# Loading the first halves of k and v through ScalarE's DMA queue

## The chip, the cores and the metric

The kernel runs on one core of one Trainium2 chip. A core has five engines with an instruction stream each: TensorE (matrix products, PE in the profile, its weight loads PEld), VectorE (DVE), ScalarE (ACT), GpSimd (POOL) and SyncE (SP). Transfers between device memory and the on-chip memory run on 16 DMA engines; an instruction of SyncE or of ScalarE issues them, and the profile shows these issues as SPq and ACTq. The metric is the device time of one execution in microseconds. Lower is better.

## What is computed

Two parts follow each other. The first is a linear attention with a cosine weight (cosFormer), for 8 batches, 8 heads, 576 positions and 64 features per head:

```python
theta = pi / 2 * arange(S) / S
phi(x) = concat(relu(x) * cos(theta), relu(x) * sin(theta))   # 64 -> 128 features
kv  = einsum('bhsf,bhsd->bhfd', phi(k), v)
z   = sum over positions of phi(k)
num = einsum('bhsf,bhfd->bhsd', phi(q), kv)
den = einsum('bhsf,bhf->bhs',  phi(q), z) + 1e-6
x   = (num / den), heads side by side: 4608 x 512
```

The second is a feed-forward layer on these 4608 rows: `h = x @ w_in` (512 to 2048), `g = max(0.01 h, h)`, `out = g @ w_out` (2048 to 512). Inputs and output are float32; the kernel multiplies in float16.

## The kernel before

The positions of a batch are split into 512 main ones (4 per partition, on 128 partitions) and a tail of 64. Each batch goes through the same steps: load q, k and v; build the features of k and q (`k_part`, `q_part`, on VectorE or ScalarE); form kv and its column of sums on TensorE (`kv_mm`); transpose the features of q; multiply them with kv and divide (`num_half`, `divide`); transpose the result x; and run the two products of the feed-forward layer over it. Batch 0 and batch 1 are written out by hand, from batch 2 on a list sorted by position (`line`, `put`) sets the order, with seven products in place of eight for 2 x 2 blocks of the feed-forward layer. Nothing reorders the program: each engine works through its instructions in the order in which they are written, and waits where an input is not there.

The change concerns the start. There all loads stand on SyncE, in this order: q of batch 0 in two halves (four heads each), first half of k, first half of v, the tails of k and of v (two transfers each), second half of k, second half of v, then eight transfers of w_in, and w_out and batch 1 after them. A half is 128 partitions x 4 heads x 4 positions x 64 features in float32, 512 KB.

While these are under way, TensorE runs 28 blank matmuls (`idle(14, ps_idle)`, line 169). VectorE and ScalarE prepare constants: the tables cos_t and sin_t (ScalarE, lines 214 and 215) are a column of every q and k feature. Then the order written out by hand for batch 0 is:

- VectorE: the features of q's first four heads (positions j = 0 and 2), of the second four heads (the same), of all heads for j = 3; then the features of k's first four heads for j = 0 to 2, the copy of v's first four heads to float16 (`v_main`), the features of k's tail, one half of v's tail.
- ScalarE: the features of q for j = 1, two copies of transposed q out of PSUM, the features of k's first four heads for j = 3, one half of v's tail, a third copy, and the copy of kv (`kv_half`, line 322).
- TensorE: the transposes of q (`q_transpose`, line 365, each over all eight heads), with blank matmuls after the first two; 18 blank matmuls; kv of the first four heads (lines 289 and 298); then, after the copy of kv, `num_half`, the same for the second four heads, the transposes of x and the first product of the feed-forward layer (`ffn1`, line 459).
- GpSimd: the copy of v's second four heads, then most of the casts of w_in to float16 (line 248).

The staging buffers of q, k and v for batch 0 (`stage`, three buffers) are given on to w_out's first two quarters and to batch 1's q once they have been read. ScalarE issues no DMA before the stores at the very end of the kernel.

Of the kernel before, what the change touches and what calls it, by code (L numbers as in the profile page):

```python
# [18 lines left out]
def kernel(  # L19
# [14 lines left out]
    nc = tc.nc  # L34
# [45 lines left out]
    ACT, DVE, POOL = nc.scalar, nc.vector, nc.gpsimd  # L80
# [3 lines left out]
    def staged(shape, name, soon=False):  # L84
        p, tag = (early, "early") if soon else (stage, "stage")
        return p.tile(shape, dt.float32, name=name, tag=tag)

    def load_main(nm, src, b, parts=(0, 1), soon=False):

        if parts[0] == 0:  # L90
            st[nm, b] = staged([P, H, J, D], f"{nm}st", soon)
        lo, hi = 4 * parts[0], 4 * parts[-1] + 4
        nc.sync.dma_start(
            st[nm, b][:, lo:hi],
            src[b, lo:hi, 0:MAIN, :].rearrange("h (p j) d -> p h j d", j=J),
        )

    def load_kvtail(nm, src, b):

        t = kvtail.tile([P, H // 2, D], dt.float32, name=f"{nm}tl", tag="kvtail")  # L100
        v4 = src[b, :, MAIN:S, :].rearrange("(c o) p d -> o p c d", o=2)
        for o in range(2):
            nc.sync.dma_start(t[o:P:2], v4[o])
        st[nm + "t", b] = t
# [10 lines left out]
    def load_k(b):  # L115
        load_main("k", k, b)
        load_kvtail("k", k, b)

    def load_v(b):
        load_main("v", v, b)  # L120
        load_kvtail("v", v, b)
# [20 lines left out]
    def load_w2(i):  # L142
        t = staged([P, 4, DM], "w2st", i > 1)
        nc.sync.dma_start(t, w2v[i])
        st["w2", i] = t

    load_main("q", q, 0, (0,))
    load_main("q", q, 0, (1,))
    load_main("k", k, 0, (0,))
    load_main("v", v, 0, (0,))  # L150
    load_kvtail("k", k, 0)
    load_kvtail("v", v, 0)
    load_main("k", k, 0, (1,))
# [943 lines left out]
    for b in range(2, NG):  # L1097
        at_, eng, s0 = AT[min(b, 5)], ENG[min(b, 5)], top[b] if b > 3 else 0
# [53 lines left out]
```

## Time and profile before

| what | value |
|---|---|
| median of 3 runs | 272.06 us |
| lowest and highest | 271.58 and 272.49 us |
| profiled execution, span from first to last instruction | 272.0 us |
| TensorE busy | 264.6 us (97%) |
| VectorE, ScalarE busy | 201.0 us, 200.7 us (74% each) |
| bytes moved by DMA | 57.05 MB, mean 210 GB/s |
| granted TensorE clock | 1.000 of full speed |

The page gives no other time of the profiled execution than its span. In a row of the order of time stand the start in us, the duration in us, the engine, the line of the kernel, the operation, the output and inputs by name, their shapes, how many instructions were merged (x8), and in brackets the idle time of the engine before it and what ended that. In a row of a table by stretches stand the stretch, its length, busy time and count of an engine, the granted clock, the mean busy share of the DMA engines and GB/s. In a row of DMA issues stand what is loaded, the issuing queue, the count, the size of one and the time from issue to landing.

### The profile page before, as it was taken

What the parts mean: (1) busy time and instruction counts of PE and PEld (TensorE: products, weight loads), DVE (VectorE), ACT (ScalarE), POOL (GpSimd) and SP (SyncE); (2) the same over time, 40 slices, a digit from 0 to 9 for tenths busy, and PEclk for the clock granted to TensorE, in tenths of its full rate; (3) what the DMA queues carried; (4) which work ended last, traced back from release to release, by engine and by line L of the source; (5) the groups of instructions that cost most, each with busy time, mean ns of one, the idle gap of its engine ahead of it and who ended that gap; (6) DMA issues with size and microseconds to landing.
All of it is one profiled execution on the core that took longest, in us unless ns stands there. A gap on an engine that the chain in (4) does not pass through costs nothing.

```text
span 272.0 us, 6597 instructions
## 1 busy us (share of the span) xinstructions
PE 264.6 (97%) x2660; PEld 226.8 (83%) x2660; DVE 201.0 (74%) x444; ACT 200.7 (74%) x331; POOL 10.1 (4%) x21
## 2 busy tenths in 40 slices
PE   8999999999999999999999999999999999999994
PEld 5876555665898979889999999999999989999983
DVE  5774589797986797899779696978577757645652
ACT  6756556696878898798899789978966657766621
POOL 1055101000000000000000000000000000000000
PEclk9999999999999999999999999999999999999999
DMA  6999989998999959997999699967274312200314
GB/s 228 318 374 413 398 291 361 368 267 254 309 208 342 175 178 264 312 172 228 259 280 161 183 276 275 181 212 155 62 149 144 61 41 96 80 0 2 154 39 118
DMA packets 87150, 57.05 MB, mean 210 GB/s; under 512 B 56656, under 2 KB 82256, under 8 KB 86608
## 3 DMA queue, kind: packets, MB, share of 16 engines
q1 hardware_dynamic: 86816, 56.37, 78.1%
q8 instruction: 21, 0.34, 0.5%
q10 hardware_dynamic: 304, 0.26, 0.4%
q14 instruction: 9, 0.07, 0.1%
HBM read 36.70 MB, written 9.44 MB: 170 GB/s over the span
## 4 chain that ended last, share of the span: by engine, by line
PE 69%; DMA 3%; DVE 2%; ACT 2%; issue 1%; ACTq 0%; DVEq 0%
PE ps_o L890 31%; PE ps_h L785 27%; PE ps_h L495 3%; DMA qst<-in_q_dram 3%; PE ps_h L890 3%; PE ps_num L380 2%; PE ps_kv L289 2%; DVE gs L254 1%; PE ps_kv L298 0%; ACT g L798 0%; PE ps_xt L445 0%; ACT g L812 0%; DVE xw L254 0%; ACT qp L238 0%; DVE xs L396 0%
## 5 line engine op out<-in xcount | busy, mean ns | idle before, releaser
L890 PEld LDWEIGHTS <-g 128*128 128x128 f16 x640 | 62.5, 98 | 7.3 <-DVE g L251 0.2
L251 DVE TENSOR_TENSOR u<-ps_h,u 128x512 f32<-128x512 f32 x52 | 35.8, 688 | 25.7 <-PE ps_h L785 22.9
L890 PE MATMUL ps_o<-w,g 128*128 128x256 f16 x352 | 51.2, 273 | 0.0
L785 PEld LDWEIGHTS <-w 128*128 128x128 f16 x416 | 44.5, 114 | 1.2
L785 PE MATMUL ps_h<-xT,w 128*128 128x256 f16 x288 | 43.3, 273 | 0.0
L785 PEld LDWEIGHTS <-wa 128*128 128x128 f16 x312 | 34.0, 113 | 2.0 <-DVE xw L254 0.9
L812 ACT ACTIVATE g<-u 128x1024 f16<-128x1024 f32 x26 | 27.5, 1058 | 10.9 <-DVE u L251 10.8
L798 ACT ACTIVATE g<-ps_h 128x512 f16<-128x512 f32 x52 | 31.2, 602 | 5.7 <-PE ps_h L785 5.7
L805 ACT COPY u<-ps_h 128x512 f32<-128x512 f32 x52 | 30.4, 585 | 5.4 <-PE ps_h L785 5.4
L890 PE MATMUL ps_o<-wb,g 128*128 128x256 f16 x232 | 33.5, 273 | 0.0
L785 PE MATMUL ps_h<-xw,wa 128*128 128x256 f16 x208 | 31.3, 273 | 0.6 <-DVE xw L254 0.6
L890 PEld LDWEIGHTS <-gs 128*128 128x128 f16 x256 | 24.9, 98 | 2.9
L908 ACT COPY ob<-ps_o 128x512 f32<-128x512 f32 (+1 forms) x32 | 17.9, 561 | 9.2 <-PE ps_o L890 9.0
L495 PE MATMUL ps_h<-xT,w 128*128 128x512 f16 (+1 forms) x104 | 24.7, 363 | 0.0
L396 DVE TENSOR_TENSOR xs<-ps_num,rden 128x512 f16<-128x512 f32 x28 | 19.4, 691 | 1.0
L890 PE MATMUL ps_o<-w,gs 128*128 128x256 f16 x120 | 17.8, 273 | 0.0
L251 DVE TENSOR_TENSOR ob<-ps_o,ob 128x512 f32<-128x512 f32 (+1 forms) x22 | 14.9, 675 | 3.7 <-ACT ob L908 1.4
L890 PE MATMUL ps_o<-wb,gs 128*128 128x256 f16 x120 | 17.5, 273 | 0.0
L254 DVE TENSOR_TENSOR gs<-g 128x1024 f16<-128x1024 f16 x16 | 11.0, 689 | 8.3 <-ACT g L812 8.1
L795 ACT COPY ps_h<-ps_h 128x512 f32<-128x512 f32 x26 | 14.9, 572 | 2.0 <-PE ps_h L785 1.1
L785 PE MATMUL ps_h<-xw,w 128*128 128x256 f16 x104 | 15.6, 273 | 0.0
L785 PE MATMUL ps_h<-xT,wa 128*128 128x256 f16 x104 | 15.6, 273 | 0.0
(113 smaller groups left out, 408.6 us busy)
## 6 DMA issues: line engine op xcount, KB each, us to landing
qst<-in_q_dram SPq DMA_DIRECT2D x7, 1024.0 KB, 7.0
out_dram<-ob SPq DMA_DIRECT2D x14, 512.0 KB, 2.8
kst<-in_k_dram SPq DMA_DIRECT2D x6, 1024.0 KB, 8.3
vst<-in_v_dram SPq DMA_DIRECT2D x6, 1024.0 KB, 7.1
w1st<-in_moe_w_in_dram SPq DMA_DIRECT2D x8, 512.0 KB, 9.4
w2st<-in_moe_w_out_dram SPq DMA_DIRECT2D x4, 1024.0 KB, 13.8
kst<-in_k_dram SPq DMA_DIRECT2D x4, 512.0 KB, 7.5
vst<-in_v_dram SPq DMA_DIRECT2D x4, 512.0 KB, 7.8
```

The costliest lines, as they stand in the source:

```text
L251: nc.vector.tensor_tensor(out=o, in0=a, in1=b, op=ALU.add)
L254: nc.vector.tensor_tensor(out=o, in0=a, in1=b, op=ALU.subtract)
L289: nc.tensor.matmul(ps[:, n * NE : (n + 1) * NE - 1], lhsT=kpm[:, h, j, :], rhs=vmain[:, h, j, 0 : NE - 1], start=(n == 0 and j == 0), stop ...
L396: nc.vector.tensor_tensor(out=xs, in0=ps[:, :, 0 : 4 * NE].rearrange("p a (b e) -> p a b e", e=NE)[:, :, :, 0:D], in1=rden.rearrange("p (a ...
L495: nc.tensor.matmul(ps[:, lo:hi], lhsT=w1[m // 4][c // 2][:, c % 2, m % 4 : 512 : 4], rhs=st["xT", g][:, c, lo:hi], start=(c == 0 and lo == 0),
L785: nc.tensor.matmul(bank[:, p], lhsT=w(c), rhs=st["xb", g][n][:, c], start=(fresh and p == 0 and c == 0), stop=(c == 1), skip_group_check=True,
L795: nc.scalar.copy(bank1[bj], bank1[bi])
L798: nc.scalar.activation(st["g" + nm, g][:, 2 * t : 2 * t + 2], bank1[bi], AF.Lrelu)
L805: nc.scalar.copy(st["u", g, t][:, n], bank1[bi])
L812: nc.scalar.activation(st["gt", g][:, :, 1, 2 * t : 2 * t + 2], st["u", g, t], AF.Lrelu)
L890: nc.tensor.matmul(bank, lhsT=st[G2[n], g][:, m, pair * P : (pair + 1) * P], rhs=W2[n](m), start=(fresh and m == 0), stop=(m == NH - 1), s ...
L908: nc.scalar.copy(o_at(g, half_, col, pair), bank_of(bi, pair, pair is None))
```

## The change

`load_main` gets a parameter for the engine that issues the transfer, and the loads of the first halves of batch 0's k and v name ScalarE:

```diff
-    def load_main(nm, src, b, parts=(0, 1), soon=False):
+    def load_main(nm, src, b, parts=(0, 1), soon=False, eng=nc.sync):
 
         if parts[0] == 0:
             st[nm, b] = staged([P, H, J, D], f"{nm}st", soon)
         lo, hi = 4 * parts[0], 4 * parts[-1] + 4
-        nc.sync.dma_start(
+        eng.dma_start(
             st[nm, b][:, lo:hi],
             src[b, lo:hi, 0:MAIN, :].rearrange("h (p j) d -> p h j d", j=J),
         )
...
     load_main("q", q, 0, (0,))
     load_main("q", q, 0, (1,))
-    load_main("k", k, 0, (0,))
-    load_main("v", v, 0, (0,))
+    load_main("k", k, 0, (0,), eng=ACT)
+    load_main("v", v, 0, (0,), eng=ACT)
     load_kvtail("k", k, 0)
     load_kvtail("v", v, 0)
     load_main("k", k, 0, (1,))
```

On SyncE the two transfers are gone from between q's second half and k's tail; the rest keeps its order. On ScalarE they become the first two instructions, ahead of the table load for cos_t and sin_t. Sizes, buffers and the work of TensorE, VectorE and GpSimd are the same.

## The prediction

> **What bounds the kernel now.** I read stretches of TensorE first, then the order of time in the first 36 us on every engine, then the landing times of the first loads.
>
> ```profile
> 7.00:12.80 5.80, 5.78 (x81) 1.00 1.04 319
> 12.80:18.50 5.70, 4.83 (x77) 1.00 1.02 361
> 18.50:35.00 16.50, 16.50 (x97) 1.00 1.04 402
> 35.00:64.00 29.00, 28.18 (x274) 1.00 1.01 302
> 64.00:260.00 196.00, 195.42 (x2041) 1.00 0.75 179
> ```
>
> These are stretches of the span with TensorE's busy time, its granted clock, the DMA engines' share and GB/s. TensorE is the bound: from 18.5 to 260 us it idles 0 + 0.82 + 0.58 = 1.4 us. So a delay of its work near 18 us reaches the end, less what the few waits of its own swallow. The DMA engines are full from 2 us on (share 1.00 and more), so in the start a load can come earlier only if another comes later. The rows of TensorE and of its weight loads (start, us, engine, line):
>
> ```profile
> 1.05 6.03 PE L166 MATMUL ps_idle<-blank 128*128 128x256 f16 x28 [1.05 <-DVE blank L162]
> 6.92 0.61 PE L365 MATMUL ps_qt<-ident,qp 128*128 128x128 f16 x8
> 9.58 2.13 PE L166 MATMUL ps_kvh<-blank 128*128 128x256 f16 x18
> 11.54 0.67 PE L289 MATMUL ps_kvh<-vmain,kpm 128*128 128x65 f16 x16
> 12.24 0.29 PE L298 MATMUL ps_kvh<-vtail,kpt 128*128 128x130 f16 x2
> 13.25 0.67 PE L416 MATMUL ps_numh<-kv,qpT 128*128 128x65 f16 x16 [0.29 <-ACT kv L322]
> 35.77 0.62 PE L365 MATMUL ps_qt<-ident,qp 128*128 128x128 f16 x8 [0.25 <-DVE qp L240]
> ...
> 6.79 0.56 PEld L365 LDWEIGHTS <-qp 128*128 128x128 f16 x8
> 15.40 0.29 PEld L289 LDWEIGHTS <-kpm 128*128 128x128 f16 x7 [0.24 <-issue]
> 17.79 0.58 PEld L459 LDWEIGHTS <-w 128*128 128x128 f16 x6 [0.41 <-POOL w L248]
> ```
>
> TensorE begins with 28 blank matmuls, which need no data and end about 7.0. Then come the transposes of batch 0's q, 18 blanks, the first products of k and v at 11.54, and the rest. Up to 12.8 it is never short of an instruction: k's landing is covered by blanks and by q's transposes. This is what the change has to beat.
>
> **The change, part by part.** First what the moved loads do today (start, us of issue, queue; then VectorE; then, each from a short window of the DMA view, KB and us from issue to landing, in the order q first half, q second half, k first half, v first half):
>
> ```profile
> 0.73 1.02 SPq L93 DMA_DIRECT2D qst<-in_q_dram  x2
> 1.80 0.51 SPq L93 DMA_DIRECT2D kst<-in_k_dram  x1
> 2.35 0.51 SPq L93 DMA_DIRECT2D vst<-in_v_dram  x1
> 6.67 2.91 SPq L93 DMA_DIRECT2D vst<-in_v_dram  x1
> ```
> ```profile
> 4.58 0.35 DVE L240 TENSOR_SCALAR qp<-qst,cos_t 128x256 f16<-128x256 f32 x1 [1.75 <-DMA qst<-in_q_dram]
> 5.83 0.35 DVE L240 TENSOR_SCALAR qp<-qst,cos_t 128x256 f16<-128x256 f32 x1
> 6.10 0.35 DVE L240 TENSOR_SCALAR qp<-qst,sin_t 128x256 f16<-128x256 f32 x1
> 7.28 0.48 DVE L240 TENSOR_SCALAR qp<-qst,sin_t 128x512 f16<-128x512 f32 x1
> 9.12 0.35 DVE L240 TENSOR_SCALAR kpm<-kst,cos_t 128x256 f16<-128x256 f32 x1 [1.36 <-DMA kst<-in_k_dram]
> 10.71 0.69 DVE L248 CAST vmain<-vst 128x1024 f16<-128x1024 f32 x1
> ```
> ```profile
> qst<-in_q_dram SPq DMA_DIRECT2D x1, 512.0 KB, 3.8
> qst<-in_q_dram SPq DMA_DIRECT2D x1, 512.0 KB, 4.5
> kst<-in_k_dram SPq DMA_DIRECT2D x1, 512.0 KB, 7.3
> vst<-in_v_dram SPq DMA_DIRECT2D x1, 512.0 KB, 8.2
> ```
>
> Today the queue is served about in order: q's halves land at 4.5 and, issued near 1.27, at 5.8; k's at 1.80 + 7.3 = 9.1; v's at 2.35 + 8.2 = 10.55. VectorE works on q from 4.58 to 7.76, then idles 1.36 us for k. That idle is all that an earlier k could remove, and TensorE does not wait on it.
>
> *SyncE's queue.* Two issues of 0.51 us go; the k and v tails and the second halves of k and v are issued 1.1 us earlier. I cost this at nothing. Their order in the queue stays, and the 2.91 us issue of v's second half shows that the queue fills and the engine waits, so transport and not issuing sets their landing. If this cover were gone, the tails would land up to 1.1 us earlier, which ends below (the wait for the tail of v).
>
> *ScalarE.* It issues two loads ahead of its first work:
>
> ```profile
> 2.33 1.28 ACT L214 ACT_TABLE_LOAD   x1 [2.33 <-DVE ones L226]
> 3.83 0.28 ACT L215 ACTIVATE sin_t<-pos,zero 128x6 f32<-128x6 f32 x1
> 11.52 0.51 ACT L221 ACTIVATE vtail<-vtl,odd 128x256 f16<-128x256 f32 x1 [1.23 <-DMA vtl<-in_v_dram]
> 12.82 0.38 ACT L322 CAST kv<-ps_kvh 128x260 f16<-128x260 f32 x1
> ```
>
> At SyncE's 0.51 us each the two issues take from about 0.75 to 1.8; ScalarE waits for its inputs until 2.33 anyway. So nothing, with 0.5 us to spare; were each 1.3 us longer, sin_t (ready 4.11) would still only just pass q's 4.58. What waits behind them is the table load and sin_t, and VectorE's first q work needs those.
>
> *The transport.* This is the term that counts. All four loads are now pending from about 0.75, q on one queue, k and v on the other. How two queues share the engines is not in this trace, where only one works at a time here. Bounds: if SyncE's queue went first, q's second half lands at 5.8 as now; if all four end together, it lands with the fourth of them. For that, the bytes moved from 2 us to each landing of today (first row q's first half, then q's second, k's, v's):
>
> ```profile
> 2.00:4.53 2.53, 1.00 0.91 306
> 2.00:5.80 3.80, 1.00 0.94 322
> 2.00:9.10 7.10, 1.00 0.98 319
> 2.00:10.55 8.55, 1.00 1.01 325
> ```
>
> 2.53 us x 306 is 0.77 MB for the first 0.52 MB; 1.22 MB for 1.05; 2.26 for 1.57; 2.78 for 2.10. A landing thus comes when 0.2 to 0.7 MB more than its own and its forerunners' bytes have moved. Four halves are 2.10 MB: with 0.2 MB more, at 320 GB/s, that is 7.2 us, so 9.2; with 0.7 MB it is v's 10.55. I take equal shares and 9.5 for q's second half, nearer to the row of the third load (9.1) since q's queue starts a little ahead. Its first half and k's would land near 6 us.
>
> The Trainium skill, DMA: Bandwidth & Descriptors, section "Queues, rings and completion order", says that each DMA engine goes round robin between the queues that hold work, a packet at a time. By that rule the halves of q and of k and v end in pairs, as I take it; its section "Issuing engines are not separate DMA queues" adds that issuing from several engines saves only issue time, which speaks against a gain here. No run here yet shows either.
>
> *What follows on VectorE and TensorE.* The first transpose needs batch 0's first q slice for all heads, so q's second half: today 5.83, two operations, done at 6.45, 0.65 after landing. The transposes then load at 6.79, when the blanks are through. After: 9.5 + 0.65 + 0.05 (as from the end of kv's copy above, 13.20, to 13.25) = 10.2, or 3.4 later. The stretch from there to the k and v products is TensorE's own work without a gap (6.79 to 11.54), so they start at 14.95. VectorE runs beside it: k follows q in its order, so it starts at 9.5 + 1.93 (5.83 to 7.76) = 11.4, and v's cast, 1.59 + 0.6 after that (9.12 to 10.71, and the cast), ends at 13.6, before 14.95. That k lay there since 6 us helps nobody: VectorE is in order and q stands ahead.
>
> *What swallows part of the 3.4.* One row more, of GpSimd:
>
> ```profile
> 14.18 1.17 POOL L248 CAST vmain<-vst 128x512 f16<-128x512 f32 x2 [12.31 <-DMA vst<-in_v_dram]
> ```
>
> ScalarE's copy of the first kv today starts at 12.82, though TensorE was done at 12.53; ScalarE had idled 1.23 us for the tail of v and came late to it. With all of TensorE 3.4 later that wait is gone: 0.29. At 15.40 the weight load has waited 0.24, for v's second half by GpSimd's cast that ends at 15.35, and at 17.79 for w_in's cast; both hang on bytes, which arrive as before. The first absorbs 0.24; of the second 0.33 count (17.79 against 17.24 + 2 x 0.11, the pace of the matmuls). The wait of 0.25 at 35.77 is for batch 1's q, also set by transport: 0.25. Sum 1.11. The waits of 1.15 us left after that (1.40 less 0.25) follow VectorE and buffers that TensorE itself releases, so they move along.
>
> Sum: 272.0 + 3.4 - 1.1 = **274.3 us**. The profiled execution's span is 272.0, the median of the runs 272.06, so I add nothing between them. With q's second half at 9.1 it is 273.9, at 10.55 it is 275.35.
>
> **The rivals.**
>
> *TensorE goes cold (slower still).* After its blanks it would stand idle from 7.1 to 10.3, 3.2 us. The trace has no such gap after the start, but it has both speeds:
>
> ```profile
> L166 PE MATMUL ps_idle<-blank x36: 272/421/421, 1.1 to 8.6; 128*128 128x256 f16 x36
> L166 PE MATMUL ps_kvh<-blank x26: 270/272/273, 9.6 to 14.5; 128*128 128x256 f16 x26
> ```
>
> The same blank takes 421 ns in the first microseconds and 272 later; by starts, 28 from 1.05 to 6.9 are 0.21 us apart and 18 from 9.58 to 11.54 0.11. At the slow pace the 18 blanks and the 8 between the transposes would cost 26 x 0.10 = 2.6 us more, less if the pace comes back midway, as it did after some 5.5 us at the start. That gives 275.8 to 276.9; it decides if the gap is long enough. For it speaks the length; against it, that blanks and transposes stand right behind the gap. The Trainium skill, TensorE: Matmul & The Clock Gate, section "Why this matters for your kernels", warns of gaps over about 3 us, which this would just be; no run here shows that limit.
>
> *No change: q keeps its place.* If SyncE's queue is served ahead, or ScalarE's issues start late, q's second half lands by 7.2, and 7.2 - 6.1 = 1.1 is just what the waits swallow. Then k arrives about as today: 272.0, between 271.5 and 272.8. For it: q's issue is first. Against it: ScalarE has nothing to do ahead of 2.33.
>
> *Faster: two queues move more bytes.* The rate at the start is 320 GB/s, 402 later. If two queues lifted the start to 402 and q still landed by 6.1, then the tail of v, v's second half and w_in's first quarter came ahead of TensorE, and the waits of 0.29 + 0.24 + 0.33 + 0.25 would go: 270.9. Equal shares at 402 do not suffice: 2.3 MB / 402 is 5.7 us, so 7.7 and 0.5 us lost. It decides at q's second half by about 6.5; against it stands that the DMA share there is already 0.91 to 1.01.
>
> *The two queues merge in order of issue.* Then q's second half is third, at 9.1: 273.9, inside my own case.
>
> **How the numbers follow.** My case 0.58, own range 273.2 to 275.6; cold TensorE 0.17; no change 0.16; faster 0.09. The likeliest gives 274.3. The range of 271.9 to 276.9 leaves out the faster case, the low third of no change and the top of the cold case, some 0.19. About 0.3%, 0.8 us, is what a measurement can tell from no change. Faster by more: 0.10; within: 0.14; slower: 0.76.
>
> **What would show it.** Right: VectorE's second q half starts after 9 us, k's first operation follows without idle, TensorE shows a wait for qp of 2 to 4 us after the first blanks, and the transposes of batch 1's q, at 35.77 today, start near 38.1. The waits at 15.40 and 17.79 vanish. Wrong: the two q landings stay at 4.5 and 5.8, or blanks at 421 ns after the gap, or v's second half and w_in landing at other times than today, since then the swallowed 1.1 is something else.

## The result and the profile after

The changed kernel takes 275.68 us (median of 4 executions, 275.20 to 276.25), the kernel before 272.27 us beside it (271.58 to 273.14). The ratio is 1.0112, 95% interval 1.0081 to 1.0144: slower by about 1.1%, or 3.1 us (the two medians differ by 3.4). Forecast were 274.3 us and a rise of 2.3; 275.68 is just above the prediction's own case, 273.2 to 275.6, and inside its whole range, 271.9 to 276.9.

Two things have to be known for the numbers below. First, in every execution of which both are listed, the time is 1.74 to 1.92 us above the span. So the profile of the kernel before, with a span of 272.0, is of an execution of about 273.8 us, 1.7 above the median. A second profile of the kernel before (experiment 5) has a span of 270.5 and a time of 272.34, and shifts are measured against that one where it is named. Second, the kernel before ran beside the experiments on four chips, with medians between 272.05 and 272.56.

The loads, of the changed kernel: the issues on ScalarE with the table load behind them (start, us, queue), then, from short windows of the DMA view, KB and us from issue to landing.

```profile
0.74 0.49 ACTq L93 DMA_DIRECT2D kst<-in_k_dram  x1
1.27 0.58 ACTq L93 DMA_DIRECT2D vst<-in_v_dram  x1
2.33 1.28 ACT L214 ACT_TABLE_LOAD   x1 [2.33 <-DVE ones L226]
```
```profile
qst<-in_q_dram SPq DMA_DIRECT2D x1, 512.0 KB, 5.0
kst<-in_k_dram ACTq DMA_DIRECT2D x1, 512.0 KB, 5.4
...
qst<-in_q_dram SPq DMA_DIRECT2D x1, 512.0 KB, 7.4
vst<-in_v_dram ACTq DMA_DIRECT2D x1, 512.0 KB, 7.8
```

The halves land in pairs: q's first at 0.73 + 5.0 = 5.7 and k's at 0.74 + 5.4 = 6.1; q's second, issued near 1.25, at 8.65 and v's at 1.27 + 7.8 = 9.1. Before, q's halves landed at 4.5 and 5.8. ScalarE's own start is untouched, its table load stands at 2.33 as before.

VectorE and TensorE, in the order of time of the changed kernel:

```profile
5.81 0.35 DVE L240 TENSOR_SCALAR qp<-qst,cos_t 128x256 f16<-128x256 f32 x1 [2.98 <-DMA qst<-in_q_dram]
8.68 0.35 DVE L240 TENSOR_SCALAR qp<-qst,cos_t 128x256 f16<-128x256 f32 x1 [1.73 <-DMA qst<-in_q_dram]
10.53 0.35 DVE L240 TENSOR_SCALAR kpm<-kst,cos_t 128x256 f16<-128x256 f32 x1
```
```profile
6.53 0.39 PE L365 MATMUL ps_qt<-ident,qp 128*128 128x128 f16 x4
9.36 0.56 PE L365 MATMUL ps_qt<-ident,qp 128*128 128x128 f16 x4 [2.44 <-DVE qp L240]
9.71 1.06 PE L166 MATMUL ps_idle<-blank 128*128 128x256 f16 x4
13.45 2.13 PE L166 MATMUL ps_kvh<-blank 128*128 128x256 f16 x18
15.41 0.67 PE L289 MATMUL ps_kvh<-vmain,kpm 128*128 128x65 f16 x16
38.32 0.61 PE L365 MATMUL ps_qt<-ident,qp 128*128 128x128 f16 x8
```

VectorE now waits for q's second half, and k, which has lain there for four microseconds, is taken without a wait at 10.53: the wait was moved from k to q. TensorE does the four transposes that the first half of q allows and then stands 2.44 us. From there its pace is about half: four blanks take 1.06 us from first start to last end, 0.60 before:

```profile
7.36 0.60 PE L166 MATMUL ps_idle<-blank 128*128 128x256 f16 x4
```

In stretches (length, busy time of TensorE, granted clock, DMA share, GB/s) the changed kernel reads:

```profile
7.00:12.80 5.80, 3.44 (x25) 0.71 1.11 358
12.80:18.50 5.70, 5.67 (x87) 1.00 1.06 399
```

Before, the first of these had 5.78 us busy, 81 matmuls and a clock of 1.00. The granted clock of 0.71 is new: after the gap TensorE ran slow until about 13.4 us. Batch 1's transposes start at 38.32, 2.55 later than in the first profile of before (35.77) and 3.18 later than in the second (35.14, below). From there to the last products the difference of 3.18 grows by 0.18 only.

### The profile page after: what moved, and what is told of

Same layout as the page of the kernel before. It is cut to its first block, busy times and chain, and to the rows that moved or that the text cites. A ratio compares the mean times of both kernels' runs of the same rounds, so it can differ in the third digit from the quotient of the medians.

```text
span 274.4 us, 6596 instructions
## 1 busy us (share of the span) xinstructions
PE 265.3 (97%) x2660; PEld 227.7 (83%) x2660; DVE 203.3 (74%) x444; ACT 201.1 (73%) x331; POOL 10.8 (4%) x21
## 4 chain that ended last, share of the span: by engine, by line
PE 69%; DMA 3%; DVE 2%; ACT 2%; issue 1%; ACTq 0%; DVEq 0%
PE ps_o L890 31%; PE ps_h L785 27%; PE ps_h L495 3%; DMA qst<-in_q_dram 3%; PE ps_h L890 3%; PE ps_num L380 2%; PE ps_kv L289 2%; DVE gs L254 1%; PE ps_kv L298 0%; ACT g L798 0%; PE ps_xt L445 0%; ACT g L812 0%; DVE xw L254 0%; ACT qp L238 0%; DVE xs L396 0%
```

## The experiments

Experiments 1 to 4, 5 to 7, 8 to 10, and 11 ran on one chip each, beside executions of the kernel before. No experiment leaves out any of the computation. Each result is the median, then the ratio to the kernel before with its 95% interval in brackets. A profile shows one execution of a kernel, and executions of one kernel differ.

### 1 and 9: TensorE kept busy through the gap

```diff
-    idle(14, ps_idle)
+    idle(26, ps_idle)
```

> The changed kernel with 52 blank matmuls ahead of q's transposes instead of 28 (24 more, about 2.6 us at the quick pace of 0.108 us each), so that TensorE has work through most of the 2.4 us in which it waits for q's second half. Theory A (late landing of q's second half, and on top of it the slow clock from 9.4 to 13.4 us, worth 4.09 - 2.45 = 1.6 us on TensorE): the blanks after the gap take 272 ns again, the 18 blanks start near 12.0 instead of 13.45, and the time falls by about 1.2 to 1.6 us, to 274.2 (about 1.006 of the kernel before). Rival B (the slow clock is hidden behind VectorE and ScalarE, which need that time anyway): the blanks are quick but the products of k and v still start near 15.4, and the time stays at 275.7 (1.011).

> The changed kernel with 52 instead of 28 blanks ahead of q's transposes, again, to price the slow clock against the changed kernel on the same chip. Theory A: 0.7 to 1.2 us below the changed kernel (1.007 to 1.008 of the kernel before). Rival B (the slow clock hides behind VectorE, ScalarE): the same as the changed kernel within 0.3 us.

The first gave 274.61 us, 1.0083 (1.0051 to 1.0114); the second, beside the changed kernel on the same chip (275.19), 274.31, 1.0075 (1.0054 to 1.0097). The blanks after the gap are quick in both (272 to 273 ns in the median). The profile of the second:

```profile
8.90 0.35 DVE L240 TENSOR_SCALAR qp<-qst,cos_t 128x256 f16<-128x256 f32 x1 [1.59 <-DMA qst<-in_q_dram]
...
9.06 0.91 PE L365 MATMUL ps_qt<-ident,qp 128*128 128x128 f16 x8
12.02 2.13 PE L166 MATMUL ps_kvh<-blank 128*128 128x256 f16 x18
37.05 0.61 PE L365 MATMUL ps_qt<-ident,qp 128*128 128x128 f16 x8
```

TensorE reaches the 18 blanks at 12.02 instead of 13.45, though q's second half came 0.2 us later, and is 1.91 us behind the kernel before at batch 1's transposes instead of 3.18. In the first run the 18 blanks also start at 12.00, but the products that follow waited 0.74 us for VectorE, and the shift was 3.00. By time both lie 0.9 to 1.1 us below the changed kernel: theory A, at a price a little under the 1.2 to 1.6 us expected first. The intervals of the two ratios overlap; what separates them is that all six executions of the second (274.01 to 274.76) lie below those of the changed kernel in experiment 8 that have the low clock (275.51 to 277.08). Two thirds to three quarters of the loss remain with the clock at full speed; they belong to the late landing.

### 8: the changed kernel again

> The changed kernel again, beside the kernel with 24 more blanks on the same chip. Theory A (late landing and slow clock): q's second half lands near 8.7, the blanks behind the gap take 421 ns, 1.011 of the kernel before. If the landing differs from execution to execution, this shows it.

275.19 us, 1.0114 (1.0082 to 1.0146). Its six executions, with the mean granted clock of TensorE over the span:

| time, us | 274.36 | 274.66 | 274.87 | 275.51 | 275.82 | 277.08 |
|---|---|---|---|---|---|---|
| clock | 1.000 | 1.000 | 1.000 | 0.991 | 0.991 | 0.987 |

The slow pace comes in some executions and not in others. Where it is missing the kernel takes 274.4 to 274.9, about as with the added blanks; where it is there, 275.5 to 277.1. All four executions of the first comparison had it (0.991 to 0.994). The profile is of one without it:

```profile
8.63 0.35 DVE L240 TENSOR_SCALAR qp<-qst,cos_t 128x256 f16<-128x256 f32 x1 [1.63 <-DMA qst<-in_q_dram]
...
9.31 0.40 PE L365 MATMUL ps_qt<-ident,qp 128*128 128x128 f16 x4 [2.38 <-DVE qp L240]
9.54 0.60 PE L166 MATMUL ps_idle<-blank 128*128 128x256 f16 x4
11.75 2.13 PE L166 MATMUL ps_kvh<-blank 128*128 128x256 f16 x18
```

The same landing and the same gap as in the first profile of the changed kernel, but 2.44 us from the end of the gap to the 18 blanks (9.31 to 11.75) instead of 4.09 (9.36 to 13.45): the slow clock costs 1.65 us on TensorE.

### 2: k alone on ScalarE's queue

```diff
-    load_main("v", v, 0, (0,), eng=ACT)
+    load_main("v", v, 0, (0,))
```

> Only k's first half goes through ScalarE's queue; v's stays on SyncE. Theory A (even sharing of bytes): q's first half and k land together near 5.7 as in the changed kernel, q's second half then has the engines nearly to itself and lands near 7.3; TensorE waits about 1 us, stays at the quick clock, and the waits behind swallow most of it: 272.3 to 273.0 (1.000 to 1.003). Rival C (a transfer on ScalarE's queue costs by itself, in proportion): half of the change's 3.4 us, 274.0 (1.006), with q's second half landing as late as 8.65.

273.20 us, 1.0028 (1.0005 to 1.0052). The rows of the order of time:

```profile
7.67 0.35 DVE L240 TENSOR_SCALAR qp<-qst,cos_t 128x256 f16<-128x256 f32 x1 [0.61 <-DMA qst<-in_q_dram]
...
8.35 0.40 PE L365 MATMUL ps_qt<-ident,qp 128*128 128x128 f16 x4 [1.35 <-DVE qp L240]
35.66 0.61 PE L365 MATMUL ps_qt<-ident,qp 128*128 128x128 f16 x8
```

q's second half lands near 7.65, a microsecond before its place in the changed kernel, since only k's bytes go ahead of it. TensorE waits 1.35 us and 0.52 of it is left at batch 1's transposes. That is theory A, with q's second half and the time a little later than expected; half of the whole loss, as rival C had it (1.006), is outside the interval.

### 3: q and k, v exchanged between the queues

```diff
-    load_main("q", q, 0, (0,))
-    load_main("q", q, 0, (1,))
-    load_main("k", k, 0, (0,), eng=ACT)
-    load_main("v", v, 0, (0,), eng=ACT)
+    load_main("q", q, 0, (0,), eng=ACT)
+    load_main("q", q, 0, (1,), eng=ACT)
+    load_main("k", k, 0, (0,))
+    load_main("v", v, 0, (0,))
```

> The other way round: q's two halves go through ScalarE's queue, k and v stay on SyncE's. Theory A (two queues share evenly, whichever engine issued): q's first half lands near 5.7, the second near 8.7, TensorE waits 2.4 us and goes slow, 275.7 (1.011). Rival D (SyncE's queue is served ahead of, or more than, ScalarE's): q lands later than in the changed kernel, second half at 9.5 or more, 276.5 and up. Rival E (ScalarE's queue is served ahead): q lands as in the kernel before, at 4.5 and 5.8, and the time is 272.3 or less.

276.43 us, 1.0145 (1.0109 to 1.0181), with a clock of 0.994 in all four executions. The landings:

```profile
kst<-in_k_dram SPq DMA_DIRECT2D x1, 512.0 KB, 5.2
qst<-in_q_dram ACTq DMA_DIRECT2D x1, 512.0 KB, 6.1
...
vst<-in_v_dram SPq DMA_DIRECT2D x1, 512.0 KB, 7.9
qst<-in_q_dram ACTq DMA_DIRECT2D x1, 512.0 KB, 8.4
```

Again in pairs, but the half on SyncE's queue leads by 0.9 us in the first pair and about 0.5 in the second; in the changed kernel, where q is on SyncE's queue, it leads by 0.4 in both. So in these two profiles sharing is close to even with a small lead for SyncE's queue (part of rival D), and here the lead falls to k: VectorE starts on q's second half at 9.75. Rival E is out.

### 4: one queue, k between the halves of q

```diff
     load_main("q", q, 0, (0,))
-    load_main("q", q, 0, (1,))
     load_main("k", k, 0, (0,))
+    load_main("q", q, 0, (1,))
     load_main("v", v, 0, (0,))
```

(against the kernel before)

> SyncE alone again, but k's first half is issued between the two halves of q. Theory A (what costs is that k's bytes go ahead of q's second half, not that there are two queues): q's second half is third in line and lands between 7.3 (1.57 MB and the 0.2 MB of the first landings at 320 GB/s, from 2 us) and 9.1 (third landing of today); TensorE waits 0.8 to 2.6 us: 272.5 to 275.7 (1.001 to 1.012), by its landing. Rival C (ScalarE's queue costs by itself): no more than 272.3 and the second half of q before 7.

273.26 us, 1.0056 (1.0023 to 1.0089). ScalarE issues nothing here, and the picture is that of experiment 2:

```profile
7.86 0.35 DVE L240 TENSOR_SCALAR qp<-qst,cos_t 128x256 f16<-128x256 f32 x1 [2.09 <-DMA qst<-in_q_dram]
...
8.53 0.40 PE L365 MATMUL ps_qt<-ident,qp 128*128 128x128 f16 x4 [1.36 <-DVE qp L240]
```

What costs is that bytes of k go ahead of q's second half; a second queue is one way to do that and an order in one queue another. Rival C falls. In 2 of its 10 executions the clock was 0.992 and 0.994, and these took 276.21 and 275.37, which raises the ratio, against 272.89 to 273.52 for the rest; in experiment 2 it was 1 of 12 (274.64 against 272.85 to 273.40). A gap of 1.35 us seems enough now and then: together 3 of 22 executions, against 1 of 76 of the kernel before.

### 5: the kernel before, once more

> The kernel before, unchanged, for a second profile of it. In the experiments k's, v's and w_in's loads landed 1 to 2 us earlier than in the first profile of before, with one queue (k's first half between q's halves: k at 5.9) as with two. Theory F (that first profile was a slow execution of the loads): here k's first half lands near 7.3 instead of 9.1, v's near 9.2, w_in's first transfer near 14.7 instead of 16.5, and batch 1's q near 33 instead of 34.8. Rival G (moving k ahead or to another queue speeds the loads up): the landings are as in the first profile, 9.1, 10.5, 16.5 and 34.8.

272.27 us, 0.9993 (0.9961 to 1.0025).

```profile
8.84 0.35 DVE L240 TENSOR_SCALAR kpm<-kst,cos_t 128x256 f16<-128x256 f32 x1 [1.06 <-DMA kst<-in_k_dram]
...
9.04 2.13 PE L166 MATMUL ps_kvh<-blank 128*128 128x256 f16 x18
...
17.70 0.60 PE L459 MATMUL ps_h<-xT,w 128*128 128x256 f16 x4 [0.24 <-ACT xT L437]
35.14 0.61 PE L365 MATMUL ps_qt<-ident,qp 128*128 128x128 f16 x8
```

k lands near 8.8, close to the 9.1 of the first profile: rival G for k. Later loads lie between the two theories: VectorE takes batch 1's q at 33.86, against 34.83 in the first profile. And the start of w_in's products waits for ScalarE's copy of x here, and not for w_in's cast as in the first profile, and batch 1's transposes wait for nothing. So two of the waits that the prediction let swallow the delay were of that one execution.

### 6 and 10: GpSimd's casts held back

```diff
     v_main(0, 6, 8, POOL)
+    gate = const.tile([P, 1], dt.float16, name="gate")
+    nc.gpsimd.tensor_copy(gate, st["kpm", 0][:, 7, 1, F - 1 : F])
```

In 6 beside the 52 blanks, in 10 on the changed kernel alone.

> The changed kernel with the 24 more blanks, and a tiny copy on GpSimd between its casts of v and of w_in that reads the last of VectorE's features of k's second four heads: the w_in casts then begin behind that work instead of beside it. Without it VectorE's operations on 256 elements took 0.69 to 0.77 us there instead of 0.35 while GpSimd was casting, and TensorE stood 0.74 + 0.27 + 0.20 us for VectorE. Theory H (the casts beside it slow VectorE down, and that ate what the quick clock gave): the four operations shorten to 0.35, the waits of TensorE go, and the time falls by 0.8 to 1.2 us against the kernel with the blanks alone, to 273.5 (1.004 to 1.005). Rival J (VectorE is slow there for another reason, or GpSimd's later casts are waited for by the first products with w_in): still 274.6 (1.008) or more.

> The changed kernel, 28 blanks, with only GpSimd's w_in casts held behind VectorE's features of k's second four heads. In the changed kernel two of these four operations took 0.70 us beside the casts, but VectorE was done with them at 16.24, ahead of the products of k's second heads at 18.05. Theory K (there TensorE at the slow clock sets the pace, VectorE's slowing is hidden): within 0.3 us of the changed kernel. Theory H (the casts beside VectorE cost here too): 0.5 us or more below it.

The last of the four VectorE operations in the first run of experiment 1, and in experiment 6:

```profile
16.86 0.69 DVE L240 TENSOR_SCALAR kpm<-kst,sin_t 128x256 f16<-128x256 f32 x1
```
```profile
15.63 0.34 DVE L240 TENSOR_SCALAR kpm<-kst,sin_t 128x256 f16<-128x256 f32 x1
```

Three of the four shorten to 0.34, and TensorE's waits for VectorE go. But the time does not fall: 274.74 us, 1.0083 (1.0053 to 1.0113), as without the gate, so J and not H by the time. Experiment 9, without a gate, had no wait of 0.74 either, so a wait of that size does not come in every execution. Experiment 10 is even slower than the changed kernel, 277.18, 1.0181 (1.0148 to 1.0214), which neither K nor H expected. In its profile q's second half is taken at 9.36, and five of six executions have the low clock. With the gate q's second half came at 9.12 and 9.36, without it at 8.63 to 8.90, and no load was touched. The gated profiles also lose time later. Against the second profile of before, batch 1's transposes are 2.00 us late in 6 and 3.68 in 10; the product that waits for VectorE's xw (at 97.22 there) is 2.57 and 4.29 late. In the changed kernel the two are 3.18 and 3.36. Why is open. So the gate changes more than the casts, and these two experiments do not settle what the casts beside VectorE cost in time: the shorter operations are shown, their price is not.

### 7: fewer blanks in the kernel before

```diff
-    kv_half(0, 0, "t", 9)
+    kv_half(0, 0, "t", 3)
```

> The kernel before, all loads on SyncE, with 6 instead of 18 blanks between q's transposes and the first products of k and v. Theory F (k and v land early enough in most executions that these blanks, and not the landing, set the start of the products): the products start near 10.9 instead of 11.5, bound by VectorE's cast of v, the copy of kv by the tail of v, and the time falls by 0.3 to 0.8 us, 271.6 to 272.0 (0.997 to 0.999). Rival G (k lands at 9.1 and v's tail at 11.5 as in the first profile): 272.3 (1.000).

272.25 us, 1.0020 (0.9987 to 1.0053). Rival G: the products start at 11.23, after a wait of 1.49 us for VectorE's cast of v. In the kernel before the blanks cost nothing that the time shows; they fill a wait for k and v. The profile is of an execution of 274.83 us. Four of the twelve took 274.1 to 275.1, two of them with a clock of 0.993.

### 11: an order fitted to the landings

One queue as in experiment 4, k's first features between the halves of q on VectorE and ScalarE, and the 18 blanks moved ahead of the transposes:

```diff
-    idle(14, ps_idle)
+    idle(23, ps_idle)
...
+        if hg == 0:
+            for j in range(3):
+                k_main(0, j, DVE, DVE, 0, 4)
+            k_main(0, 3, ACT, ACT, 0, 4)
...
-    kv_half(0, 0, "t", 9)
+    kv_half(0, 0, "t")
```

> A version made from what the runs showed: SyncE alone, k's first half between the halves of q as in the kernel with one mixed queue (there all four halves had landed by 9.3 us instead of 10.2 to 10.6), and the work fitted to it: VectorE and ScalarE take k's first features between the two halves of q, and the 18 blanks ahead of the products of k and v stand ahead of q's transposes. Theory A: q's second half lands near 7.8, the transposes start near 8.5 without a slow clock, the products of k and v near 11.2 as in the kernel before, the first kv is copied 0.3 us sooner: 0.0 to 0.5 us below the kernel before, 0.998 to 1.000. If the place of q's second half binds even so: 0.5 us or more above it, 1.002 to 1.004.

272.09 us, 0.9983 (0.9954 to 1.0011): not to be told from the kernel before, which is theory A by time. But q's second half was expected near 7.8, and in the profile (an execution of 273.48 us) it lands at 9.6, later than in experiment 4. Yet TensorE is only 0.78 us behind at batch 1's transposes (35.92 against 35.14):

```profile
9.60 0.35 DVE L240 TENSOR_SCALAR qp<-qst,cos_t 128x256 f16<-128x256 f32 x1 [2.07 <-DMA qst<-in_q_dram]
```

In this profile a late second half of q costs less: k's work stands ahead of it, and blanks keep TensorE busy. Both were changed at once, so how much each saves is not shown; that k had to wait behind q on VectorE was probably part of the price.

The loads of this kernel and of experiment 4 stand in the same order, and q's second half is issued at 1.80 us in both. From issue to landing, experiment 4 first:

```profile
qst<-in_q_dram SPq DMA_DIRECT2D x1, 512.0 KB, 6.0
```
```profile
qst<-in_q_dram SPq DMA_DIRECT2D x1, 512.0 KB, 7.8
```

v's first half, issued at 2.35 in both, lands at 9.25 and 10.95. So the order of the loads alone does not set when they land.

### The runs side by side

| kernel | q's second half taken, us | TensorE's wait there, us | behind the second profile of before at batch 1's transposes, us | ratio |
|---|---|---|---|---|
| before (5) | 5.85 | none | 0 | 0.9993 |
| k alone (2) | 7.67 | 1.35 | 0.52 | 1.0028 |
| one queue, mixed (4) | 7.86 | 1.36 | 0.71 | 1.0056 |
| 52 blanks (9) | 8.90 | filled with blanks | 1.91 | 1.0075 |
| changed, full clock (8) | 8.63 | 2.38 | 2.13 | 1.0114 (all six) |
| changed, slow clock | 8.68 | 2.44 | 3.18 | 1.0112 |
| exchanged (3), slow clock | 9.75 | 2.42 | 4.09 | 1.0145 |

## Why the prediction was right, and where it was not

**The bound and the path.** Right. TensorE carries any delay of the start to the end: in the changed kernel the 3.18 us at batch 1's transposes are still 3.36 at the last products. k's landing was covered before, q's second half was not. Most of the expected signs came: k without a wait, a wait of TensorE for qp, no gain anywhere. One did not: VectorE takes q's second half at 8.68, not after 9 us. And two of the signs that were to show the prediction wrong came as well. The blanks after the gap took 421 ns, and GpSimd's casts of v's second half and of w_in start at 13.35 and 14.71, against 14.18 and 16.57 in the first profile of before (13.91 and 15.22 in the second).

**ScalarE and SyncE's issues.** Right. Two issues of 0.49 and 0.58 us end at 1.85, the table load stays at 2.33.

**The transport.** Even sharing was right, the landing too late. Forecast 9.5 with bounds from 9.2 to 10.55; measured 8.65, and 8.6 to 9.4 in the six profiles with these loads. The term that failed is the "0.2 to 0.7 MB" said to have moved beyond a landing's own bytes: by 9.1, with all four halves landed, 7.1 us x 331 GB/s = 2.35 MB had moved, 0.25 MB more than theirs. The 0.7 was taken from k's and v's landings in one execution on one queue, and does not carry over; experiments 4 and 11, with the fourth half at 9.25 and 10.95, show that a landing also moves between profiles with the same loads. The Trainium skill, DMA: Bandwidth & Descriptors, section "Queues, rings and completion order", has the DMA engines go round robin between queues; the pairs at 5.7 and 6.1 and at 8.65 and 9.1 agree, the leads of 0.4 us there and of 0.5 to 0.9 in experiment 3 show that it is only nearly even.

**TensorE's delay.** 3.4 us were forecast at the transposes. The landing gave 2.4, the wait of TensorE; the slow clock added 1.65 behind it. The term was a microsecond too large, and another of 1.65 was missing from the sum. That batch 1's transposes start at 38.32, close to the 38.1 forecast, is luck: these two errors have opposite signs. A reading failed too: not all transposes wait for q's second half. Four of the first eight need its first half only and ran at 6.53.

**The cold clock.** This was a rival at 0.17, and it is what happened in all four executions of the first comparison and three of six of the second. Its price, 2.6 us for the whole stretch and less if the pace comes back, was sized rightly as a bound: 1.65 on TensorE, and 275.5 to 277.1 against 274.4 to 274.9 in time. Its chance was too low: taking the gap of a kernel from its profile and a mean clock under 0.995 as the sign, a gap of 2.4 us did it in 7 of 10 executions of the changed kernel and one of 1.35 in 3 of 22. The Trainium skill, TensorE: Matmul & The Clock Gate, section "What's actually happening", tells of a window of about 3.4 us that runs free of the kernel; by that rule the same gap would meet the window now one way and now another, as experiment 8 shows. The traces lean the same way: the first 28 blanks took 4.86 us in the profile of experiment 8, without the slow pace, and 5.64, 5.98 and 5.77 in those with it (changed kernel, experiments 3 and 10), so the start became quick later there; four profiles do not prove it. The gap of about 3 us that the same page of the Trainium skill allows, in its section "Why this matters for your kernels", is too long by these runs.

**What the waits swallow.** Forecast 1.11; from the 18 blanks to batch 1's transposes the shift against the first profile of before falls from 3.87 (13.45 less 9.58) to 2.55, by 1.32, and against the second from 4.41 (13.45 less 9.04) to 3.18, by 1.23. The sum is about right, but its parts at 17.79 and 35.77 were waits of one execution; experiment 5 does not have them. In experiment 8 only 0.58 are swallowed (from 11.75 less 9.04, 2.71, to 2.13): there TensorE waits 0.19, 0.27 and 0.20 us for VectorE.

**The base and the size.** "I add nothing between them" was wrong in its ground: the span of 272.0 and the median of 272.06 agree by accident, as that execution took about 1.7 us more than the median and its span is about 1.8 below its time. The base came out right, but two of the waits in the sum belonged to that execution. A rise of 2.3 was forecast; it is 3.1 by the ratio. The step of the sum that failed is the slow clock, put at nothing in the likeliest case: in the executions of experiment 8 with the full clock the rise is 2.1 to 2.6 (274.36 to 274.87 against 272.25), and the slow clock is the rest. That the forecast 2.3 lies in 2.1 to 2.6 is in part luck. With the measured landing the prediction's own sum gives 8.65 + 0.70 - 6.79 - 1.11 = 1.45. Experiment 8 shows about that against the first profile of before (37.27 less 35.77, 1.50); but that profile is of an execution 1.7 us above the median, and against the second it is 2.13. The landing put too late made up for the base taken from that profile.

**The rivals.** "No change" and "faster" fell with the landing: q's second half at 8.65 is past the 7.2 that the waits could swallow. Two queues did not lift the start's rate enough: 331 GB/s from 2 to 9.1 us in the changed kernel, 319 and 322 in the two profiles of before.

## What to carry to other kernels

When loads compete for full DMA engines, do not count on a second issuing queue for more bandwidth: here it moved 331 GB/s against 319 and 322, and took its share from whatever was first in line. Ask which bytes are needed first, and keep later ones out of the way until those have landed. A short stall of TensorE can cost more than its length: check the granted clock and the pace of the stretch behind it, over several executions, since the slow pace comes in some and not in others.

## What the runs showed of the hardware

- The same program with the same gap ran behind it at the full pace in one execution (2.44 us to the 18 blanks) and at half in another (4.09). None of 20 executions with 52 blanks (experiments 1, 6 and 9), and none of 12 of the kernel of experiment 11 (gap 1.84 us in its profile), had a mean clock under 0.995. Of the kernel before, beside the experiments, 1 of 76 had, and of the kernel with fewer blanks (a wait of 1.49 us) 2 of 12.
- The granted clock did not show the slow pace at the start: in the first profile of before it reads 1.00 from 3 to 6 us, where the blanks take 421 ns. There the pace is read from the blanks themselves.
- The same four loads on one queue, in the same order, landed at different times: q, k, q, v by 9.25 us in the profile of experiment 4 and by 10.95 in that of experiment 11; q, q, k, v by 10.55 and 10.15 in the two profiles of before. From 7.00 to 12.80 us the DMA engines moved 356 GB/s in experiment 4 and 294 in experiment 11. The cause was not found.
- VectorE's operations on 128 x 256 elements took 0.69 to 0.78 us while GpSimd was casting beside them, 0.34 to 0.35 without a cast or where they began ahead of it, and values between where the two overlap in part; experiment 6, which moves the casts, has three of four at 0.34. What that is worth in time is not shown.
